# Causal attention and a gated unit on one core: a table of engine orders and choices replaced, 22 masks on GpSimd become 5

## The chip, the core and the metric

The kernel runs on one core of a Trainium2 chip. A core has five engines that run side by side, each through its own list of instructions in a fixed order: PE (TensorE, matrix products; its weight loads are a row of their own, PEld), DVE (VectorE), ACT (ScalarE), POOL (GpSimd) and SP (SyncE, which here issues the DMA transfers). An instruction waits until the instructions on other engines that it depends on have finished, and everything behind it on its engine waits with it. Products land in PSUM, eight banks of 512 fp32 per partition; PE writes them, ACT and DVE read them. In this kernel POOL works on SBUF alone.

The metric is device time in microseconds. Profile times are counted from the start of the profiled span.

## The reference

What is computed, with the setup and the types left out:

```python
def _attn_ref(q, k, v, s):                       # q, k, v: 8 x 8 x 576 x 64, s: 8 x 8 x 576
    scores = scale * np.matmul(q, k.transpose(0, 1, 3, 2))
    causal = np.triu(np.ones((S, S), dtype=bool), k=1)
    cum = np.cumsum(np.maximum(s, 0.0), axis=-1)
    bias = -(cum[:, :, :, None] - cum[:, :, None, :])
    scores = np.where(causal, -1000000000.0, scores + np.minimum(bias, 0.0))
    attn = np.exp(scores - np.max(scores, axis=-1, keepdims=True))
    attn = attn / (np.sum(attn, axis=-1, keepdims=True) + 1e-09)
    return np.matmul(attn, v)

def _moe_ref(x, w_val, conv_w, w_out):           # x: 8 x 576 x 512, the heads side by side
    xp = np.concatenate([np.zeros((B, K - 1, D)), x], axis=1)
    gate_pre = np.zeros((B, S, D))
    for k in range(K):                           # K = 5 taps
        gate_pre += conv_w[k][None, None, :] * xp[:, k:k + S, :]
    gate = 1.0 / (1.0 + np.exp(-gate_pre))
    return (gate * (x @ w_val)) @ w_out
```

## The kernel before

**Tiling.** The eight batches of eight heads are 32 units n = 4 b + p, each a batch b and a pair of heads p. The 576 positions fall in five key blocks of 128, 128, 128, 128 and 64. Because the bias is a difference of two cumulated sums, its row part falls away in the normalisation and its column part is a factor on v: `w` = exp(cum), and `vprime` writes Vp = v * w with a last column for the sum of each row.

**The steps of a unit.** q and k are loaded (`ld_q`, `ld_k`, the last 64 positions by `ld_t`), cast to bf16 (`c_q`, `c_k`), turned on PE (`qt`, `qq`, `tt`) and copied out of PSUM to the tiles QKT (`qe`, `te`). The scores come in three steps of 1024 columns for the two heads (`s0`, `s1`, `s2`, and `s4` for the last key block), each followed by one exp on ACT (`e0`, `e1`, `e2`, `e4`) into one of three buffers P. Step 0 holds the diagonal blocks. `av0` and `av` multiply P with Vp, 30 products of 65 columns; `rec` and `nm` normalise; `xt` turns the result and `xe` copies it out of PSUM to xT. The convolution is one start and three sums on a tile gp (`t1` to `t4`): on DVE a sum is one instruction, on POOL it needs a product first (`p2` to `p4`, into one of two buffers pr; such a product is sometimes made by ACT) and then an addition. `th` is the tanh of the gate, `val` the product with w_val, `glu` joins the two. `out` (128 rows each) is the product with w_out, `oe` copies it out of PSUM and `st` stores it. The last four units are split into a first part of 384 positions and a second of 192, with steps `u0` to `u3` and exps `f0` to `f3`, so that their products, sums and tanhs are of 384 and 192 columns.

**Two ways to mask.** The future positions of a diagonal block have to become zero. Either POOL writes zeros into P after the exp (`mk`, for the split units also `ml` for the second part: one affine select), or PE adds a large negative number to the scores ahead of the exp (`future`: two products with the tiles `fut`, one for each half of the rows, into the banks of step 0). Which one a unit gets follows from the table: where it names `mk.n`, unit n is masked on POOL, and else on PE.

**What sets the order.** One long table, `ORDER`, lists every step once, as name, engine and slots: `e` in `c_k.2:A:2` is A for ACT, V for DVE, G for POOL, T for PE, S for SP, and the rest names a PSUM bank, two banks, or a buffer. A loop at the end of `main_path` walks through it and emits each step; nothing reorders afterwards. So the table says for each engine in which order its work stands, which engine does a step that several can do, and in which bank or buffer. `wu` are products of the identity whose result nobody reads; they fill PE. All loads but the first two of k, and all stores, are issued by SP in the order of the table. The tiles `vst` of v are two, one for even and one for odd batches, so a load of v for batch b waits for the four `vp` of batch b - 2.

At the end `chk0` and `chk` reduce the reciprocals to a few flags on DVE, `cnt` counts them on PE, and every engine reads the count to decide whether `general_path`, a slower form that these inputs never need, has to run.

Of the kernel before, what the change touches and what calls it, by code (L numbers as in the profile page):

```python
# [16 lines left out]
B, H, S, D = 8, 8, 576, 64  # L17
# [175 lines left out]
ld_k.0.0:A ld_q.0.0:S ld_k.0.1:A wu.0:T:0 ld_t.0:S wu.1:T:7 wu.2:T:0 wu.3:T:7 ld_s:S wu.4:T:0 ld_q.0.1:S wu.5:T:7  # L193
wu.6:T:0 ld_q.0.2:S wu.7:T:7 c_k.0.0:V ld_k.0.2:S qt.0.0.k:T:0 wu.8:T:2 c_q.0.0:V ld_v.0.1:S qe.0.0.k:A qt.0.0.q:T:1
wu.9:T:7 c_k.0.1:G qe.0.0.q:A wu.10:T:2 wu.11:T:7 s0.0:T:0+1:0 e0.0:A tt.0:T:2 ld_q.0.3:S relu:V qt.0.1.k:T:3
wu.12:T:4 ld_k.0.3:S te.0:A wu.13:T:7 scan:V mk.0:G wu.14:T:0 ld_v.0.0:S qe.0.1.k:A s1.0:T:1+2 s4.0.0:T:4+5 c_q.0.1:A
s2.0:T:6+7 wu.15:T:0 c_q.0.2:G e1.0:A qt.0.1.q:T:3 wu.16:T:0 qe.0.1.q:V wu.17:T:0 wu.18:T:0 e4.0.0:A wu.19:T:0
centre:V s0.1:T:4+5:1 ld_k.1.0:S:2 s2.1:T:2+3 e0.1:A qt.0.2.q:T:1 c_k.0.2:V decT:T:0 ld_cw:S e2.0:A qt.0.2.k:T:4
mk.1:G wu.20:T:5 ld_k.1.1:S qe.0.2.k:V wu.21:T:5 wu.22:T:5 qe.0.2.q:A s1.1:T:6+7 c_k.0.3:V e2.1:A s0.2:T:4+5:2
c_q.0.3:G ld_v.0.2:S expw:A qt.0.3.q:T:1 e1.1:A s4.0.1:T:2+3 qe.0.3.q:V vp.0.0:G qt.0.3.k:T:0 qe.0.3.k:V e4.0.1:A  # L200
ld_q.1.0:S:3 e0.2:A s2.2:T:6+7 s1.2:T:2+3 vp.0.1:G av0.0:T:0+1 e2.2:A av.0:T ld_v.0.3:S mk.2:G rec.0:V av0.1:T:4+5
e1.2:A nm.0:V av.1:T c_k.1.0:G:2 s0.3:T:6+7:0 rec.1:V s2.3:T:2+3 e0.3:A nm.1:V ld_t.1:S cwT:T:0 xt.0:T:1 c_k.1.1:G
cwc:V xt.1:T:4 e2.3:A wu.23:T:6 xe.0:V ld_q.1.1:S vp.0.2:G qq.1.1:T:0:7 t1.0:V:0 s4.0.2:T:2+3 s1.3:T:5+6 e4.0.2:A
xe.1:V c_q.1.0:A:0 s4.0.3:T:2+3 mk.3:G t3.0:V ld_v.1.2:S e4.0.3:A t1.1:V:1 e1.3:A ld_v.1.1:S av0.2:T:2+3 vp.0.3:G
av.2:T t2.0:V ld_v.1.0:S qe.1.3:A tt.1:T:5 ld_v.1.3:S qe.1.2:V p4.1:G:0 p4.0:A:1 ld_v.1.4:S ld_wv:S:4 av0.3:T:6+7
av.3:T te.1:A rec.2:V ld_t.2:S t4.1:G c_q.1.1:G nm.2:V s0.6:T:0+1:1 rec.3:V xt.2:T:5 nm.3:V e0.6:A t4.0:G s0.7:T:2+3:2
xe.2:V s2.6:T:6+7 e0.7:A qq.1.0:T:0:1 t1.2:V:2 mk.6:G p2.1:A:0 s1.6:T:2+3 t3.2:V qe.1.0:A ld_q.2:S:0 mk.7:G qe.1.1:V
e2.6:A t3.1:V s1.4:T:0+1 e1.6:A s0.4:T:6+7:0 t2.2:V ld_k.2:S:1 xt.3:T:4 e0.4:A s0.5:T:2+3:0 t2.1:G t4.2:V s2.4:T:6+7
xe.3:V wu.24:T:5 e2.4:A vp.1.0:G mk.4:G wu.25:T:5 t1.3:V:3 wu.26:T:5 wu.27:T:5 ld_wo:S:2 wu.28:T:5 e1.4:A s4.1.3:T:6+7
ld_t.3:S t3.3:V wu.29:T:5 wu.30:T:5 e4.1.3:A s1.5:T:0+1 t4.3:V wu.31:T:5 th.2:A:0 ld_q.3:S:3 vp.1.2:G av0.4:T:6+7  # L210
th.1:A:1 av.4:T t2.3:V e0.5:A vp.1.1:G cast_wv:G rec.4:V av0.6:T:4+5 nm.4:V av.6:T e1.5:A s2.5:T:2+3 rec.6:V
s1.7:T:6+7 nm.6:V e2.5:A xt.4:T:0 ld_v.2.2:S c_q.2:G:1 tt.2:T:1 xe.4:V th.0:A:2 av0.5:T:2+3 t1.4:V:2 av.5:T te.2:A
ld_v.2.4:S val.3.0:T:4 th.3:A:3 p4.4:G:1 rec.5:V val.3.1:T:1 nm.5:V e1.7:A val.1.0:T:5 glu.3.0:V t4.4:G xt.5:T:2
c_k.2:A:2 glu.3.1:V ld_v.2.1:S val.1.1:T:3 glu.1.0:V s2.7:T:6+7 glu.1.1:V qq.2.0:T:1:5 vp.1.3:G xe.5:V val.0.0:T:3
# [82 lines left out]
def main_path(ctx, tc, q, k, v, s, moe_w_val, moe_conv_w, moe_w_out, out, okcnt):  # L297
# [44 lines left out]
    Ps = kind("P", [128, 2, 1536], BF16)  # L342
# [25 lines left out]
    at = {}  # L368
# [289 lines left out]
    def tap(m):  # L658
# [15 lines left out]
        return f  # L674

    split = lambda n: ("u0", n) in at

    def thof(n):
        return ths[at["th" if ("th", n) in at else "th0", n][0]].rearrange("p (h s) -> p h s", h=2)

# [159 lines left out]
```

## Time and profile before

| what | value |
|---|---|
| device time, three runs | 187.39, 188.7, 189.65 us; median 188.7 |
| span of the profiled execution | 187.6 us, 6637 instructions; the median of the runs is 1.1 above it |
| granted TensorE clock, mean | 0.999 |
| DMA | 40.46 MB, mean 216 GB/s |
| instructions of POOL that mask | 22 (18 of 1024 elements, 4 of 256) |

The device time of the profiled execution itself is not listed apart from the three runs. Its span, first to last instruction, is the time that the profile's rows divide up, and the sum below is made on it.

In the profile a row of the groups names the line, the engine, the operation, output and inputs, the shapes and the count; then the busy time, the mean length of one, and the engine's idle time just before these instructions with what ended it. Instructions of one engine overlap a little: a row of three exps lasts less than three times the length of one. L373 is the line of a helper that makes every copy and cast, so its groups are told apart by their tiles.

### The profile page before, as it was taken

The page shows a single profiled execution, that of the slowest core. Times are in us where ns is not written, and L with a number is a line of the kernel's source. Part 1 is how long each engine was busy: PE and PEld are TensorE (multiplying, and loading weights), DVE is VectorE, ACT ScalarE, POOL GpSimd, SP SyncE. Part 2 cuts the span into 40 slices and gives each one's busy share as a digit, 9 for nine tenths or more (in the row PEclk, how much of TensorE's full clock was granted, in tenths as well). Part 3 has the DMA queues.
Part 4 walks back from the last instruction along what each step waited for, and adds up shares of the span by engine and source line. Part 5 has one row for each costly group of instructions (what it writes and reads, how often), then busy time and mean ns, then how long its engine had stood idle before and what let it go on. Part 6 is the DMA issues. An engine that isn't in the chain of part 4 may idle for free.

```text
span 187.6 us, 6637 instructions
## 1 busy us (share of the span) xinstructions
PE 170.1 (91%) x2704; PEld 113.5 (60%) x2720; DVE 163.3 (87%) x321; ACT 170.6 (91%) x230; POOL 164.5 (88%) x149
## 2 busy tenths in 40 slices
PE   6898885888899998998978999999999999999991
PEld 2556573476757765576745667586566865776560
DVE  4355999878997899999999899998989899999980
ACT  2589899899999999999999999999999999999772
POOL 5267999899999999999978999999999989899610
PEclk9999999999999999999999999999999999999999
DMA  5998999999999999999298999899541003401164
GB/s 164 274 277 246 231 225 243 343 388 341 193 232 304 277 303 258 389 270 283 71 248 184 274 333 325 193 314 247 164 162 66 3 0 115 171 3 56 61 224 175
DMA packets 62283, 40.46 MB, mean 216 GB/s; under 512 B 47333, under 2 KB 49381, under 8 KB 62250
## 3 DMA queue, kind: packets, MB, share of 16 engines
q1 hardware_dynamic: 61706, 39.49, 77.1%
q8 instruction: 22, 0.36, 0.8%
q10 hardware_dynamic: 544, 0.52, 0.8%
q14 instruction: 11, 0.09, 0.2%
HBM read 30.57 MB, written 9.44 MB: 213 GB/s over the span
## 4 chain that ended last, share of the span: by engine, by line
PE 50%; ACT 15%; SPq 9%; DMA 8%; issue 6%; POOL 5%; DVE 4%; ACTq 0%; POOLq 0%; DVEq 0%
PE bank L723 14%; PE bank L703 11%; PE bank L594 10%; ACT P L556 9%; PE bank L505 7%; DMA vst<-in_v_dram 6%; SPq L435 3%; PE bank L629 3%; PE bank L626 3%; POOL gp L673 2%; DMA first<-in_k_dram 2%; ACT th L690 2%; SPq L471 2%; ACT QKT L373 2%; SPq L467 2%
## 5 line engine op out<-in xcount | busy, mean ns | idle before, releaser
L556 ACT ACTIVATE P<-bank 128x1024 bf16<-128x1024 f32 x84 | 82.9, 1042 | 4.1 <-PE bank L505 3.0
L670 DVE SCALAR_TENSOR_TENSOR gp<-bank,cwr,gp 128x574 f32<-128x574 bf16 (+6 forms) x72 | 52.3, 740 | 0.9 <-POOL gp L673 0.5
L673 POOL TENSOR_TENSOR gp<-gp,pr 128x572 f32<-128x572 f32 (+6 forms) x36 | 45.1, 1259 | 4.4 <-DVE gp L670 1.7
L474 POOL TENSOR_TENSOR Vp<-vst,w 128x650 bf16<-128x650 f32 x32 | 40.7, 1288 | 2.8 <-DMA vst<-in_v_dram 1.8
L505 PE MATMUL bank<-QKT 64*128 64x128 bf16 (+4 forms) x592 | 37.2, 237 | 4.8 <-ACT P L556 1.8
L703 PE MATMUL bank<-xT,wv 128*128 128x288 bf16 (+2 forms) x256 | 38.5, 287 | 1.1 <-ACT P L556 0.5
L594 PE MATMUL bank<-Vp,P 128*128 128x65 bf16 x960 | 36.0, 194 | 2.4 <-POOL Vp L474 1.1
L594 PEld LDWEIGHTS <-P 128*128 128x128 bf16 x960 | 33.2, 97 | 6.8 <-issue 1.5
L723 PE MATMUL bank<-wo,glu 128*128 128x512 bf16 x128 | 34.1, 380 | 1.5 <-issue 0.5
L505 PEld LDWEIGHTS <-QKT 64*128 64x128 bf16 x592 | 19.4, 94 | 22.3 <-issue 14.6
L712 DVE SCALAR_TENSOR_TENSOR glu<-th,bank 128x288 bf16<-128x288 f32 (+2 forms) x64 | 27.5, 445 | 2.0 <-ACT th L690 0.9
L703 PEld LDWEIGHTS <-wv 128*128 128x128 bf16 x256 | 22.4, 97 | 11.0 <-issue 4.8
L654 POOL TENSOR_TENSOR pr<-xT,cwr 128x572 f32<-128x572 bf16 (+6 forms) x28 | 28.3, 1020 | 0.6 <-ACT xT L373 0.6
L373 ACT COPY QKT<-bank 128x1024 bf16<-128x1024 bf16 (+1 forms) x26 | 24.2, 966 | 3.8 <-PE bank L489 2.9
L613 DVE TENSOR_TENSOR xn<-bank,recs 128x640 bf16<-128x640 f32 (+2 forms) x36 | 26.8, 745 | 0.6
L665 DVE SCALAR_TENSOR_TENSOR gp<-xT,cwr,bank 128x576 f32<-128x576 bf16 (+2 forms) x36 | 26.4, 741 | 0.7
L579 POOL TENSOR_SCALAR_AFFINE_SELECT P<-P 128x1024 bf16<-128x1024 bf16 (+1 forms) x22 | 22.3, 1021 | 4.2 <-ACT P L556 4.2
L690 ACT ACTIVATE th<-gp,cwr 128x576 f32<-128x576 f32 x28 | 22.0, 794 | 0.1
L723 PEld LDWEIGHTS <-glu 128*128 128x128 bf16 x144 | 12.4, 98 | 13.2 <-issue 1.6
L373 ACT COPY ot<-bank 128x512 f32<-128x512 f32 x26 | 15.2, 610 | 1.5 <-PE bank L723 1.0
L626 PE MATMUL bank<-ident,xn 128*128 128x128 bf16 x164 | 14.9, 219 | 0.7 <-ACT P L556 0.3
L373 POOL CAST qkb<-qkf 128x2048 bf16<-128x2048 f32 (+1 forms) x9 | 14.4, 1619 | 0.0
(66 smaller groups left out, 174.8 us busy)
## 6 DMA issues: line engine op xcount, KB each, us to landing
out_dram<-ot SPq DMA_DIRECT2D x36, 256.0 KB, 4.3
vst<-in_v_dram SPq DMA_DIRECT2D x28, 256.0 KB, 5.9
first<-in_q_dram SPq DMA_DIRECT2D x6, 512.0 KB, 6.0
first<-in_k_dram SPq DMA_DIRECT2D x6, 512.0 KB, 6.2
qkf<-in_q_dram SPq DMA_DIRECT2D x6, 512.0 KB, 6.7
qkf<-in_k_dram SPq DMA_DIRECT2D x6, 512.0 KB, 7.3
vst<-in_v_dram SPq DMA_DIRECT2D x15, 128.0 KB, 5.4
first<-in_q_dram SPq DMA_DIRECT2D x4, 256.0 KB, 5.3
```

The lines of the kernel that those rows point to most:

```text
L373: (act.copy if e is act else e.tensor_copy)(dst, src)
L474: e.tensor_tensor(Vps[b % 2][:, :, HP[p]], vslot(b)[:, :, HP[p]], w[:, :, b * 8 + 2 * p:b * 8 + 2 * p + 2].unsqueeze(3).to_broadcast([128, ...
L505: pe.matmul(ps[:, hh, c0:c0 + nq], QKTs[b % 2][r, 1, p, k0:k0 + 128], QKTs[b % 2][r, 0, p, q0:q0 + nq], **kw)
L556: act.activation(out=Pt(n)[:, :, step * 512:(step + 1) * 512], in_=pair((f"s{step}", n)), func=AF.Exp, scale=0.125)
L594: pe.matmul(ps[:, o:o + 65], lhsT, Vps[b % 2][:, kb, 2 * p + w, :], start=(kb == 0), stop=(kb == qb))
L613: vec.tensor_tensor(xns[b % 2][:, g, p * 128:(p + 1) * 128].rearrange("t g (w d) -> t w g d", w=2), ps[:, :, :, 0:64], recs[:, n, :, g].un ...
L654: pool.tensor_tensor(pr, xTs[b % 2][:, c, 4 + lo - m:4 + hi - m], r.to_broadcast([128, hi - lo]), ALU.mult)
L670: vec.scalar_tensor_tensor(gp[:, lo:hi], xps(n, *h)[:, lo - m:hi - m], r, gp[:, lo:hi], ALU.mult, ALU.add)
L673: pool.tensor_tensor(gp[:, lo:hi], gp[:, lo:hi], prs[at[f"p{m}", n, *h][0]][:, lo:hi], ALU.add)
L703: pe.matmul(ps, wv[:, dc, c * 128:(c + 1) * 128], xTs[b % 2][:, dc, 4 + lo:4 + hi], start=(dc == 0), stop=(dc == 3))
L712: vec.scalar_tensor_tensor(glu2[:, c, o + lo:o + hi], th[:, lo:hi], 1.0, ps, ALU.add, ALU.mult)
L723: pe.matmul(bank_of(u, i), glu2[:, c, i * 128:i * 128 + 128], wo[:, c, :], start=(c == 0), stop=(c == 3))
```

## The change

The table `ORDER` is replaced. Loads and stores are issued by SP in the same sequence as before. By engine, the steps that another engine does now, or that are there in another number:

| step | before | after |
|---|---|---|
| masks on POOL, `mk` / `ml` | 18 / 4 | 5 (units 11, 17, 22, 25 and the split unit 29) / 0 |
| units whose step 0 is masked on PE, of the 28 whole ones | 10 | 24 |
| fillers `wu` on PE | 32 | 50 |
| casts `c_k.2`, `c_k.0.2`, `c_k.1.0`, `c_q.0.1` | ACT, DVE, POOL, ACT | POOL, ACT, ACT, POOL |
| tap products on POOL, whole / half | 20 / 8 | 21 / 10 |
| tap products on ACT, whole / half | 7 / 1 | 5 / 2 |
| tap sums on POOL, whole / half | 27 / 9 | 26 / 12 |
| tap sums on DVE, whole / half | 57 / 15 | 58 / 12 |
| `qe` on ACT, DVE | 26, 10 | 28, 8 |
| `oe` on ACT, DVE | 26, 10 | 28, 8 |
| `te` on ACT, DVE | 6, 2 | 4, 4 |
| `xe` on ACT, DVE | 12, 24 | 10, 26 |
| `chk0` on DVE | behind `nm.27`, among the tap sums of unit 24 | behind the last `glu` |

The first rows of the table in the diff, and what else it changes (a buffer P is now named where the first exp of a unit writes it, since its three steps no longer come in one order):

```diff
 ORDER = """
-ld_k.0.0:A ld_q.0.0:S ld_k.0.1:A wu.0:T:0 ld_t.0:S wu.1:T:7 wu.2:T:0 wu.3:T:7 ld_s:S wu.4:T:0 ld_q.0.1:S wu.5:T:7
+ld_q.0.0:S ld_k.0.0:A ld_k.0.1:A ld_t.0:S ld_s:S ld_q.0.1:S ld_q.0.2:S ld_k.0.2:S c_q.0.0:V ld_v.0.1:S c_k.0.0:V
...
-    Pt = lambda n, h=None: Ps[at["s0" if h is None else f"u{2 * h}", n][1]]
+    split = lambda n: n in splits
+
+    def Pt(n, h=None):
+        steps = ("e0", "e1", "e2") if h is None else (f"f{2 * h}", f"f{2 * h + 1}")
+        return Ps[next(at[f, n] for f in steps if (f, n) in at)[0]]
...
-            split = ("u0", n) in at
-            g = ((3, 1)[h] if split else 4)
+            g = ((3, 1)[h] if split(n) else 4)
...
+    splits = {int(name.split(".")[1]) for name, *_ in steps if name.startswith("u0.")}
```

Three places of the new order. First POOL, from its first cast of the inputs to the v of batch 0 (Vp0, from the buffer vst0). L579 is the mask; it stands in the new file on L586, L373 on L377, L474 on L478. Before:

```order
L373 CAST qkb1_103<-first_91 128x2x4x64
L579 AFFINE_SELECT P0_116<-P0_116 128x2x512
L373 CAST qkb0_102<-first_91 128x2x4x64
L579 AFFINE_SELECT P1_117<-P1_117 128x2x512
L373 CAST qkb0_102<-first_91 128x2x4x64
L474 TENSOR_TENSOR Vp0_109<-vst0_92,w_140 128x5x130 x2
L579 AFFINE_SELECT P2_118<-P2_118 128x2x512
L373 CAST qkb2_104<-qkf0_136 128x2x8x64 x2
```

and after:

```order
L377 CAST qkb1_103<-first_91 128x2x4x64
L377 CAST qkb0_102<-first_91 128x2x4x64 x2
L478 TENSOR_TENSOR Vp0_109<-vst0_92,w_140 128x5x130
L377 CAST qkb0_102<-first_91 128x2x4x64
L478 TENSOR_TENSOR Vp0_109<-vst0_92,w_140 128x5x130
L377 CAST qkb2_104<-qkf0_136 128x2x8x64
L478 TENSOR_TENSOR Vp0_109<-vst0_92,w_140 128x5x130 x2
L377 CAST qkb1_103<-qkf1_137 128x2x8x64
```

The three masks between are gone from POOL, and so the casts of q and k and the Vp of batch 0 follow one another.

The second place is POOL from the v of batch 3 (Vp1, from the buffer vst1) to the k of batch 6. `gp` is a tap sum, `pr` a tap product, the casts to qkb take q and k of later batches. Before:

```order
L474 TENSOR_TENSOR Vp1_110<-vst1_93,w_140 128x5x130 x2
L579 AFFINE_SELECT P0_116<-P0_116 128x2x512
L579 AFFINE_SELECT P2_118<-P2_118 128x2x512
L373 CAST qkb0_102<-qkf2_138 128x4x8x64
L474 TENSOR_TENSOR Vp1_110<-vst1_93,w_140 128x5x130
L579 AFFINE_SELECT P1_117<-P1_117 128x2x512
L373 CAST qkb1_103<-qkf0_136 128x4x8x64
L373 CAST qkb2_104<-qkf1_137 128x4x8x64
L673 TENSOR_TENSOR gp2_121<-gp2_121,pr0_134 128x572
L474 TENSOR_TENSOR Vp1_110<-vst1_93,w_140 128x5x130
```

and after:

```order
L377 CAST qkb2_104<-first_91 128x4x8x64
L478 TENSOR_TENSOR Vp1_110<-vst1_93,w_140 128x5x130 x4
L377 CAST qkb1_103<-qkf0_136 128x4x8x64
L377 CAST qkb0_102<-qkf1_137 128x4x8x64
L377 CAST qkb2_104<-qkf2_138 128x4x8x64
L377 CAST qkb1_103<-first_91 128x4x8x64
L680 TENSOR_TENSOR gp3_122<-gp3_122,pr1_135 128x572
L661 TENSOR_TENSOR pr0_134<-xT1_114,cwr_144 128x572
```

The four Vp of batch 3, which stood apart with three masks, three casts and a tap sum between them, are one row, and the cast of k of batch 6 (qkb1 from the tile first) has come ahead of the tap sum of unit 13 (in the new table `t4.13`, the row of gp3).

The third place is the end of DVE, from the last `glu`. `okt`, `stat` and `ok` are the flags, `okcnt` their count. Before:

```order
L712 SCALAR_TENSOR_TENSOR glu2_115<-th3_126,bank_153 128x192
L712 SCALAR_TENSOR_TENSOR glu2_115<-th1_124,bank_153 128x192
L734 TENSOR_REDUCE stat_149<-recs_141 128x1
L735 TENSOR_REDUCE stat_149<-recs_141 128x1
L745 TENSOR_SCALAR ok_148<-stat_149 128x2
L746 TENSOR_SCALAR ok_148<-stat_149 128x2
L758 TENSOR_REDUCE okcnt_58<-bank_153 1x1
```

and after:

```order
L716 SCALAR_TENSOR_TENSOR glu2_115<-th2_125,bank_153 128x192
L716 SCALAR_TENSOR_TENSOR glu2_115<-th0_123,bank_153 128x192
L716 SCALAR_TENSOR_TENSOR glu2_115<-th3_126,bank_153 128x192
L743 TENSOR_TENSOR okt_150<-cwr_144 128x20
L744 TENSOR_SCALAR ok_148<-okt_150 128x20
L738 TENSOR_REDUCE stat_149<-recs_141 128x1
L739 TENSOR_REDUCE stat_149<-recs_141 128x1
```

The last four of these rows are `chk0`; it now stands between the last `glu` and `chk`, whose five rows follow as before.

## The prediction on record

> **What bounds the kernel now.** I read the page's busy times first, then six stretches, then the waits and the chain, and last single instructions. The busy times:
>
> ```profile
> PE 170.1 (91%) x2704; PEld 113.5 (60%) x2720; DVE 163.3 (87%) x321; ACT 170.6 (91%) x230; POOL 164.5 (88%) x149
> ```
>
> Four engines are at 87 to 91%, so an average tells nothing about which one holds the end. The stretches (width, then busy time of PE, PEld, DVE, ACT, POOL with instruction counts, granted clock, DMA share, GB/s) do:
>
> ```profile
> 0.00:10.00 10.00, 8.03 (x51) 3.73 (x51) 4.61 (x15) 4.61 (x7) 4.32 (x14) 1.00 0.88 221
> 10.00:40.00 30.00, 24.56 (x453) 16.63 (x452) 24.71 (x43) 27.43 (x37) 26.36 (x24) 1.00 1.02 272
> 40.00:90.00 50.00, 47.22 (x811) 32.34 (x815) 45.73 (x84) 48.95 (x60) 49.77 (x38) 1.00 1.10 289
> 90.00:160.00 70.00, 67.00 (x1126) 45.57 (x1127) 66.41 (x120) 68.44 (x91) 67.11 (x53) 1.00 0.64 178
> 160.00:173.00 13.00, 12.95 (x198) 9.26 (x198) 12.73 (x34) 12.53 (x21) 12.35 (x16) 1.00 0.22 79
> 173.00:188.00 15.00, 10.33 (x92) 5.95 (x90) 9.10 (x30) 8.68 (x19) 4.58 (x9) 0.98 0.40 144
> ```
>
> From 40 to 90 us POOL is the fullest: it idles 50.00 - 49.77 = 0.23 us, ACT 1.05. From 90 to 160 ACT is the fullest (idle 1.56; POOL 2.89). Between 10 and 173 us ACT idles 2.57 + 1.05 + 1.56 + 0.47 = 5.65 us in all. So two engines bound the middle, POOL first and ACT about 1 us behind it. PE is the fullest only from 160 on. The loads bound the first 34 us, and the chain shows it:
>
> ```profile
> 28.08 5.99 DMA vst<-in_v_dram
> ...
> 34.23 1.28 POOL Vp L474
> 35.51 1.06 POOL P L579
> 36.61 1.11 PE bank L594 x30
> ```
>
> The v of batch 1 is issued at 28.08, lands at 34, is scaled by POOL, and then a POOL mask (L579, 1.06 us) stands between it and the PE products that need both.
>
> **The change, part by part.** The prices of the moved work are these groups (busy us, mean ns of one):
>
> ```profile
> L579 POOL TENSOR_SCALAR_AFFINE_SELECT P<-P 128x1024 bf16<-128x1024 bf16 x18 | 20.6, 1153 | 4.2 <-ACT P L556 4.2
> ...
> L579 POOL TENSOR_SCALAR_AFFINE_SELECT P<-P 128x256 bf16<-128x256 bf16 x4 | 1.7, 426 | 0.0
> ...
> L373 POOL CAST qkb<-first 128x2048 bf16<-128x2048 f32 x5 | 9.5, 1896 | 0.0
> ...
> L654 POOL TENSOR_TENSOR pr<-xT,cwr 128x572 f32<-128x572 bf16 x9 | 10.3, 1147 | 0.2 <-ACT xT L373 0.2
> ...
> L673 POOL TENSOR_TENSOR gp<-gp,pr 128x572 f32<-128x572 f32 x13 | 18.3, 1406 | 1.7 <-DVE gp L670 1.3
> ...
> L620 PE MATMUL bank<-ident 128*128 128x512 bf16 x32 | 10.7, 451 | 1.4 <-POOL ident masks.py:199 1.4
> ...
> L518 PE MATMUL bank<-fut,fut 64*128 64x512 bf16 x20 | 3.8, 376 | 0.0
> ```
>
> *Masks off POOL.* Eighteen full masks cost 20.6 us, 1.14 each; four small ones 1.7. Four full ones stay and one of 768 elements is new, which I put between 0.43 and 1.14 in proportion to its elements, at 0.9. That is 4 x 1.14 + 0.9 = 5.5 in place of 22.3, so -16.8 us. POOL takes in return one whole cast of k (1.9) and loses a half one while gaining a small one (together +1.5), and, by the table of counts, one full tap product more and one full tap sum fewer (1.15 - 1.41 = -0.3), two half products and three half sums more (about 0.64 each, between half and two thirds of the rows L654 and L673: +3.2). That is +2.9. Sum: -12.4 us, POOL from 164.5 to about 152.
>
> *Masks onto PE.* Fourteen more score groups get the pair of `fut` products. Ten pairs take 3.8 us now, 0.38 a pair with their drain. A product of 512 columns in a run takes 0.22:
>
> ```profile
> 54.27 1.73 PE bank L723 x8
> ```
>
> (1.73 / 8). The two of a pair lie on the two halves of the rows, so a pair costs 0.22 to 0.38, and the fourteen 3.1 to 5.3 us of PE. Four masks of the split steps move as well, each a pair of 128 columns, under 0.1 us. Eighteen more filler products (L620, 10.7 / 32 = 0.33 each) add 6.0 us of busy PE, and in the order all but two stand ahead of the first output products, where PE has idle time (24.56 of 30.00 busy between 10 and 40 us). I cost them at nothing; their cover is that idle time, and if it is gone they cost up to 6. PE's cover for the masks is that its groups run with drain between them; the waits say how often ACT really stands for its scores:
>
> ```profile
> ACT P L556 <- PE bank L505: 3.0, 7, 0.7
> ...
> POOL P L579 <- ACT P L556: 4.2, 2, 2.6
> ...
> DVE recs L607 <- PE bank L594: 5.0, 9, 1.4
> ```
>
> Three us in 84 exps: PE is mostly ahead of ACT. I take 0 for the masks on the path and keep +5.3 as the upper end; below nothing there is a gain, since the mask's 1.1 us leaves the path from exp to the value products (the 1.06 at 35.51 above).
>
> *ACT.* The exps and tanhs do not change in number. What moves on or off:
>
> ```profile
> L373 ACT COPY QKT<-bank 128x1024 bf16<-128x1024 bf16 x22 | 21.8, 1034 | 0.7 <-PE bank L629 0.6
> ...
> L373 ACT COPY ot<-bank 128x512 f32<-128x512 f32 x26 | 15.2, 610 | 1.5 <-PE bank L723 1.0 <-ACT ot L373 0.6
> ...
> L373 ACT CAST QKT<-bank 128x512 bf16<-128x512 f32 x6 | 3.6, 606 | 0.4 <-PE bank L480 0.4
> ...
> L373 ACT CAST qkb<-first 128x2048 bf16<-128x2048 f32 x1 | 1.9, 1898 | 0.0
> ...
> L373 ACT CAST qkb<-qkf 128x1024 bf16<-128x1024 f32 x1 | 1.0, 1037 | 0.0
> ...
> L373 ACT COPY QKT<-bank 128x512 bf16<-128x512 bf16 x4 | 2.4, 592 | 3.0 <-PE bank L489 2.9
> ...
> L652 ACT ACTIVATE pr<-bank,cwr 128x572 f32<-128x572 bf16 x4 | 3.2, 789 | 0.0
> ...
> L373 ACT COPY xT<-bank 128x576 bf16<-128x576 bf16 x7 | 4.6, 656 | 0.0
> ```
>
> One big cast leaves, one half comes: -1.90 + 1.04. Two evacuations of QKT come, one whole, one small: +1.03 + 0.59. Two of the outputs come, +1.22; two tails leave, -1.21. One copy of xT leaves, -0.66. Two whole tap products leave and a half one comes, about -0.9. Sum -0.8 us. DVE loses two output copies, two QKT copies and half a cast, gains two tails and a copy of xT: about -2.5 us, on an engine that idles 3.6 us between 90 and 160; I take nothing for it.
>
> *v of batch 3 and the SP queue.* SP issues in order. Its own timeline and POOL's:
>
> ```profile
> 85.32 0.63 SPq L731 DMA_DIRECT2D out_dram<-ot  x1
> ...
> 92.41 0.99 SPq L471 DMA_DIRECT2D vst<-in_v_dram  x2
> ...
> 91.06 1.32 POOL L474 TENSOR_TENSOR Vp<-vst,w 128x650 bf16<-128x650 f32 x1
> ...
> 98.97 1.28 POOL L474 TENSOR_TENSOR Vp<-vst,w 128x650 bf16<-128x650 f32 x1 [0.88 <-DMA vst<-in_v_dram]
> ```
>
> From 85.95 to 92.41 SP stands before the first v of batch 5, since that buffer is free only when POOL has made the last Vp of batch 3, at 91.06. Behind it in the queue is the last v of batch 4, so POOL waits for that until 98.97. The change makes all four Vp of batch 3 in one piece ahead of the casts, so the 6.5 us of SP go. What is late next is one row further in POOL's new order: the cast of k of batch 6, now ahead of the tap sum that was at 89.71. The second half of its load is issued only at 82.67 here, and such loads take 7.3 us to landing (the last number of the second row):
>
> ```profile
> 82.67 0.63 SPq L435 DMA_DIRECT2D first<-in_k_dram  x1
> ...
> qkf<-in_k_dram SPq DMA_DIRECT2D x6, 512.0 KB, 7.3
> ```
>
> So that cast starts no earlier than 82.67 + 7.3 = 90, and everything behind it on POOL waits: what POOL saves before 90 us can't be carried past that row whole. So I take the gain from ACT's idle time and none from POOL's 12.4 us as such.
>
> *The check of the sums* moves to the end of DVE's order. It costs four short instructions, the longest of them
>
> ```profile
> L734 DVE TENSOR_REDUCE stat<-recs 128x1 f32<-128x280 f32 x1 | 0.4, 437 | 0.0
> ...
> 182.37 0.17 DVE L746 TENSOR_SCALAR ok<-stat 128x2 bf16<-128x2 f32 x1
> ...
> 183.37 0.17 PE L749 MATMUL bank<-ok,onec 128*1 128x24 bf16 x1
> ```
>
> With two such reductions and two smaller ones some 1.2 us. The count that follows was ready at 182.54 and ran at 183.37 behind the last output products, so 0.8 is covered. I take 0 and keep +0.4.
>
> *The sum.* On the profiled span of 187.6: -0.8 (ACT's own work) and -1.7, which is 30% of ACT's idle 5.65 us. I choose 30% because POOL, whose fullness feeds part of those waits, is relieved before 90 us alone by the full amount, and the loads hold one place of it. That gives 185.1. The median of the three runs is 1.1 above the span, so 186.2. The ends: all of the 5.65 gone, 187.6 - 0.8 - 5.65 = 181.2, with the 1.1 182.3; and all fourteen pairs on the path at 0.38, 188.7 - 0.8 + 5.3 = 193.2.
>
> [...]
>
> **The rivals.**
>
> 1. *ACT and the loads hold it.* POOL's idle time grows and nothing else moves: 188.7 - 0.8 = 187.9. For it: ACT idles just 1.05 and 1.56 us in the two long stretches, and SP's row at 82.67. Against it: POOL idles 0.23 between 40 and 90, less than ACT.
> 2. *Slower: masks on PE ahead of the exps.* PE works in order, and the pair now sits between the scores and ACT's exp of the diagonal step. It decides from the point where PE comes to that group no earlier than ACT does; then each pair is ACT's wait. Fourteen at 0.22 to 0.38, less 0.8: 191.0 to 193.2. For it: PE has half of the chain below, and 12.95 of 13.00 us from 160 on. Against it: the 3.0 us that ACT waited in all.
>
> ```profile
> PE 50%; ACT 15%; SPq 9%; DMA 8%; issue 6%; POOL 5%; DVE 4%; ACTq 0%; POOLq 0%; DVEq 0%
> ```
>
> 3. *Much faster.* POOL was the bound through the first half and its waits end everywhere: all of ACT's idle time goes, 182.3 to 184.
>
> **How the numbers follow.** About 1% is what a measurement of this kernel can tell from no change: the three runs lie between 187.39 and 189.65. The forecast has 0.45, around 186.2 (185.0 to 187.3), four fifths of it below 186.8; rival 1 has 0.22 at 187.9, rival 2 0.20 from 190 on, rival 3 0.13. Faster by over 1%: 0.36 + 0.13 = 0.49. Within 1%: 0.09 + 0.22 + 0.04 = 0.35. Slower by over 1%: 0.16. The range from 183.0 to 190.9 leaves out half of rival 3 and a good half of rival 2, some 0.18.
>
> **What would show it.** Right: POOL's busy time near 152; L579 at five instructions; no SP wait of 6 us for Vp; ACT's idle time between 10 and 173 us about 4; ACT's waits for L505 still near 3 us. Rival 1: ACT's idle time as now, and POOL's waits on the k loads in its place. Rival 2: ACT's waits for PE by L505 or L518 over 6 us. Wrong altogether: new waits of ACT for DVE or POOL where the new order sets a step just behind its source, which no row here can show.

## The result and the profile after

The changed kernel takes 194.5 us (median of four runs, 194.04 to 195.03) against 188.62 for the kernel before on the same chip: a ratio of 1.030, interval 1.025 to 1.035. It is 5.9 us slower; the forecast was 186.2, and its range ended at 190.9. The profiled execution has a span of 193.15 us, 5.6 more than the 187.57 of before. Medians, ratios and intervals in this document are over fast runs; a run more than 1.5% above the fastest of its kernel counts as slow and is left out.

The changed kernel's page, busy time by engine:

```profile
PE 176.0 (91%) x2754; PEld 115.4 (60%) x2772; DVE 165.3 (86%) x318; ACT 170.0 (88%) x229; POOL 153.3 (79%) x138
```

POOL lost 11.2 us of work and ACT 0.6, and yet the span grew: the relief did not reach the end. The six stretches of the changed kernel (width, then busy time of PE, PEld, DVE, ACT, POOL with counts, granted clock, DMA share, GB/s):

```profile
0.00:10.00 10.00, 8.48 (x56) 4.12 (x56) 4.03 (x15) 3.86 (x5) 4.07 (x15) 1.00 0.88 223
10.00:40.00 30.00, 26.88 (x469) 17.13 (x462) 24.25 (x42) 28.51 (x38) 17.70 (x16) 1.00 1.00 275
40.00:90.00 50.00, 47.96 (x823) 32.72 (x828) 45.88 (x80) 47.84 (x62) 44.35 (x32) 1.00 1.02 281
90.00:160.00 70.00, 66.21 (x1114) 44.38 (x1116) 65.62 (x115) 66.10 (x86) 65.31 (x52) 1.00 0.65 174
160.00:173.00 13.00, 12.84 (x181) 8.77 (x180) 12.75 (x30) 12.71 (x21) 11.34 (x11) 1.00 0.28 102
173.00:188.00 15.00, 13.65 (x146) 8.24 (x147) 12.75 (x41) 10.96 (x22) 10.58 (x17) 1.00 0.38 141
```

The reader should follow ACT, the fourth of the busy times. Its idle time is 1.49 us from 10 to 40 (2.57 before), then 2.16 (1.05), 3.90 (1.56) and 0.29 (0.47): 7.84 us in place of 5.65. It gains 1.1 us early and loses 3.5 between 40 and 160. What it waits for is in the list of waits (engine, line and what ended the wait: us in all, times, longest):

```profile
ACT P L564 <- PE bank L509: 3.2, 5, 1.2
...
ACT P L564 <- PE bank L522: 1.9, 3, 0.8
...
ACT P L536 <- PE bank L522: 1.0, 3, 0.5
```

L564 and L536 are exps, L509 the scores and L522 the mask products. The exps wait 6.1 us for PE in 11 waits, 3.2 us of it for scores and 2.9 for mask products; before, they waited 3.0 for the scores, L505. The chain has moved to PE and DVE and no longer runs over SP and DMA:

```profile
PE 54%; DVE 19%; ACT 9%; issue 8%; POOL 7%; POOLq 0%; DVEq 0%; ACTq 0%
```

The rest of the loss lies behind the last work. Before, PE's branch past `general_path` (L807) began at 184.65 and the span ended 2.92 us later. In the changed kernel (L812) it began at 188.21, and the end came 4.94 us later. The branch of each engine in the changed kernel; the three numbers in ns are the shortest, the median and the longest:

```profile
L812 ACTq COMPARE_BRANCH  x1: 45/45/45, 188.1 to 188.1; - x1
L812 POOLq COMPARE_BRANCH  x1: 45/45/45, 188.2 to 188.2; - x1
L812 DVEq COMPARE_BRANCH  x1: 72/72/72, 188.2 to 188.2; - x1
L812 PEldq COMPARE_BRANCH  x1: 3898/3898/3898, 188.2 to 188.2; - x1
```

and PE's in the kernel before:

```profile
L807 PEldq COMPARE_BRANCH  x1: 358/358/358, 184.7 to 184.7; - x1
```

So the 5.6 us of span are 3.6 by which PE reaches its branch later, and 2.0 behind that.

### The profile page after: what moved, and what is told of

Same layout as the page of the kernel before. It is cut to its first block, busy times and chain, and to the rows that moved or that the text cites. A ratio compares the mean times of both kernels' runs of the same rounds, so it can differ in the third digit from the quotient of the medians.

```text
span 193.1 us, 6754 instructions
## 1 busy us (share of the span) xinstructions
PE 176.0 (91%) x2754; PEld 115.4 (60%) x2772; DVE 165.3 (86%) x318; ACT 170.0 (88%) x229; POOL 153.3 (79%) x138
## 4 chain that ended last, share of the span: by engine, by line
PE 54%; DVE 19%; ACT 9%; issue 8%; POOL 7%; POOLq 0%; DVEq 0%; ACTq 0%
PE bank L601 11%; PE bank L727 10%; PE bank L707 10%; PE bank L509 9%; DVE gp L677 6%; ACT P L564 5%; DVE gp L672 4%; POOL gp L680 3%; PE bank L633 3%; PE bank L636 3%; PE bank L627 3%; DVE glu L716 3%; DVE xn L620 2%; POOL pr L661 2%; PE bank L522 2%
## 5 line engine op out<-in xcount | busy, mean ns | idle before, releaser
L564 ACT ACTIVATE P<-bank 128x1024 bf16<-128x1024 f32 x84 | 81.7, 1043 | 5.6 <-PE bank L509 3.2
L677 DVE SCALAR_TENSOR_TENSOR gp<-bank,cwr,gp 128x574 f32<-128x574 bf16 (+5 forms) x70 | 53.2, 761 | 1.8
L478 POOL TENSOR_TENSOR Vp<-vst,w 128x650 bf16<-128x650 f32 x32 | 40.5, 1284 | 5.4 <-DVE QKT L377 3.9
L509 PE MATMUL bank<-QKT 64*128 64x128 bf16 (+5 forms) x592 | 37.8, 237 | 3.3 <-ACT P L564 2.5
L707 PE MATMUL bank<-xT,wv 128*128 128x288 bf16 (+2 forms) x256 | 37.0, 286 | 0.8 <-ACT P L564 0.6
L661 POOL TENSOR_TENSOR pr<-xT,cwr 128x572 f32<-128x572 bf16 (+6 forms) x31 | 30.4, 985 | 6.8 <-DVE xT L377 4.9
L601 PE MATMUL bank<-Vp,P 128*128 128x65 bf16 x960 | 34.2, 194 | 0.2 <-POOL Vp L478 0.2
L601 PEld LDWEIGHTS <-P 128*128 128x128 bf16 x960 | 31.9, 98 | 4.2 <-issue 1.4
L509 PEld LDWEIGHTS <-QKT 64*128 64x128 bf16 x592 | 20.1, 94 | 22.1 <-issue 15.4
L377 ACT COPY QKT<-bank 128x1024 bf16<-128x1024 bf16 (+1 forms) x28 | 25.9, 974 | 3.5 <-PE bank L493 3.3
L716 DVE SCALAR_TENSOR_TENSOR glu<-th,bank 128x288 bf16<-128x288 f32 (+2 forms) x64 | 26.1, 448 | 2.7 <-PE bank L707 1.6
L377 POOL CAST qkb<-first 128x2048 bf16<-128x2048 f32 (+1 forms) x10 | 14.0, 1402 | 8.0 <-DMA first<-in_q_dram 3.0
L377 POOL CAST qkb<-qkf 128x2048 bf16<-128x2048 f32 (+1 forms) x8 | 13.4, 1677 | 5.0 <-PE bank L484 2.9
L627 PE MATMUL bank<-ident 128*128 128x512 bf16 x50 | 15.8, 432 | 1.4 <-POOL ident masks.py:199 1.4
L377 ACT COPY ot<-bank 128x512 f32<-128x512 f32 x28 | 16.2, 606 | 0.9 <-PE bank L727 0.7
```

The lines of the kernel that those rows point to most:

```text
L377: (act.copy if e is act else e.tensor_copy)(dst, src)
L478: e.tensor_tensor(Vps[b % 2][:, :, HP[p]], vslot(b)[:, :, HP[p]], w[:, :, b * 8 + 2 * p:b * 8 + 2 * p + 2].unsqueeze(3).to_broadcast([128, ...
L509: pe.matmul(ps[:, hh, c0:c0 + nq], QKTs[b % 2][r, 1, p, k0:k0 + 128], QKTs[b % 2][r, 0, p, q0:q0 + nq], **kw)
L564: act.activation(out=Pt(n)[:, :, step * 512:(step + 1) * 512], in_=pair((f"s{step}", n)), func=AF.Exp, scale=0.125)
L601: pe.matmul(ps[:, o:o + 65], lhsT, Vps[b % 2][:, kb, 2 * p + w, :], start=(kb == 0), stop=(kb == qb))
L661: pool.tensor_tensor(pr, xTs[b % 2][:, c, 4 + lo - m:4 + hi - m], r.to_broadcast([128, hi - lo]), ALU.mult)
```

## The experiments

All times are medians beside the kernel before on the same chip; ratios are to that kernel, with a 95% interval. "Delay" below is the start of a batch's exps (those of the last key block apart) in a profiled execution less that of the same exps in the kernel before, as a mean. It compares one execution with one, and is good to about 1 us: two traces of the changed order, with the dear and the cheap branch of the next section, have delays of 3.32 and 2.25 us at the last `glu`, ahead of that branch. The trace of before is also of a long execution. In all runs whose span is on record the device time is 1.66 to 2.23 us above the span, so the span of 187.57 belongs to the longest run of before, 189.65, and against its median the delays would be some 1 us larger.

### The branch at the end

The edit is the same in both kernels: a filler becomes four products of 128 columns, the same 512 columns for PE in more instructions; in the kernel before PE comes to its branch at 184.5 us with them and at 184.65 without.

```diff
+SPLIT = (0, 1, 2, 3, 4, 5, 6, 7)
...
     def unread(e, i):
+        if i in SPLIT:
+            for j in range(4):
+                pe.matmul(bank[:, at["wu", i][0], 128 * j:128 * j + 128], ident, ident, start=True, stop=True)
+            return
```

In the kernel before (fillers 0 to 16):

> The kernel before, with its first 17 fillers each issued as four products of 128 columns and no longer as one of 512: the same PE work and order, 102 more PE instructions, so that the last branch of PE stands 5515 instructions into its program, 5413 in before and 5518 in the changed kernel. Theory 'place of the branch': the 3.9 us that PE's compare-and-branch takes at the end of the changed kernel (0.36 us in before) hangs on how many PE instructions stand ahead of it. Then this kernel's branch takes 3 to 4 us too and the time is 190.7 us, 2.1 over before (189.8 to 191.2). Rival 'the check at the end': the branch is slow because the changed kernel has its first checks (chk0) at the end, or for its data; then the branch takes 0.4 us here and the time is 188.6 (188.0 to 189.2).

In the changed kernel (fillers 0 to 7, as in the diff):

> The changed kernel with its first 8 fillers split in the same way: 48 more PE instructions, the branch at 5566. In the trace of the changed kernel a 16 KB fetch of PE instructions came about every 256 of them, the last ones after some 5288 and 5540. Theory 'place of the branch': with the branch past 5540 the next block has been fetched ahead of it, so that the branch takes 0.4 us again: 192.4 us, 2.1 under the changed kernel (191.9 to 192.9). Theory that only the count matters, the more the slower: no gain, 194.5. Rival 'the check at the end': 194.5 (194.0 to 195.0).

Measured: 190.68 us, 1.0108 (1.0057 to 1.0158), and 191.92 us, 1.0205 (1.0151 to 1.0259). Each came out where the first theory had it. PE's branch in the kernel before with 102 more instructions:

```profile
L812 PEldq COMPARE_BRANCH  x1: 4158/4158/4158, 184.5 to 184.5; - x1
```

and in the changed kernel with 48 more:

```profile
L817 PEldq COMPARE_BRANCH  x1: 445/445/445, 187.2 to 187.2; - x1
```

The same code, at the same time in the program and with the same data, takes over ten times as long with the branch behind 5515 instructions as behind 5413, and is cheap again behind 5566. That is a loss of 2.0 us by the spans, and a third of the whole. `chk0` has no part in it, as it stands early in the first of the two and late in the second. All kernels below have their branch at a place known to be cheap (behind 5566 to 5571) or dear (5515 to 5518), nearly all by split fillers. Those in the changed order are read against 1.0205 or 1.0301 accordingly, those in before's order against 1 or 1.0108.

### Masks: from GpSimd to PE, and back

First before's table with its masks as in the changed kernel.

```diff
-mk.0:G ... mk.27:G ml.28:G ml.29:G ml.30:G ml.31:G
+mk.11:G mk.17:G mk.22:G mk.25:G mk.29:G
```

> The kernel before with its masks where the changed kernel has them (units 17, 25 and the first half of 29 to GpSimd; 0 to 4, 6, 7, 9, 12 to 14, 18 to 20, 24, 27 and the second halves of 28 to 31 to PE), all else in before's order; 6 fillers split, so that the branch stands at 5517 as in the kernel with 17 split, against which it is read. Theory 'masks': the mask products on PE make the exponentials late by most of the 3.4 us that the changed kernel loses ahead of its end: +2 to +4 us over the kernel with 17 fillers split, 192.7 to 194.7 if the branch costs 2.1 us. Rival 'order': the loss comes from the new order of the engines, and the masks alone move the time by no more than 0.7 us either way, or make it shorter since GpSimd has 15 us less to do: 189.5 to 191.4 with the dear branch.

Measured: 192.98 us, 1.0249 (1.0185 to 1.0314), 2.3 us over its partner with the dear branch. The sum falls on the side of the masks, but the trace shows no delay of the exps of batches 1 to 6 (between -0.9 and +0.1 us against its partner), and then one wait: ACT stands 1.25 us ahead of the first exp of unit 31, which starts at 164.46, 1.6 later than in the partner. PE had stood still there, for a mask that this kernel adds on GpSimd:

```profile
L594 PE MATMUL bank<-Vp,P 128*128 128x65 bf16 x960 | 35.7, 194 | 2.3 <-POOL P L579 1.1
```

So the run put a price on two things at once. The next leaves the three added masks on PE:

```diff
-mk.17:G mk.25:G mk.29:G
```

> The kernel before with 20 masks taken from GpSimd to PE (units 0 to 4, 6, 7, 9, 12 to 14, 18 to 20, 24, 27 and the second halves of 28 to 31), as in the changed kernel, and none put on GpSimd in their place: in the run that had three more there, the only late wait against its partner was 1.36 us ahead of the first exponential of unit 31's first half. 13 fillers are split, so that the branch stands at 5571, where it was cheap. Theory 'order': PE's mask products are covered in before's order, and GpSimd's 20 masks less shorten nothing: 188.6 (188.0 to 189.2). Rival 'masks': the products cost time wherever they stand, 190.4 to 191.5.

Measured over 12 runs: 190.24 us, 1.0059 (1.0029 to 1.0089), 1.1 us, between the two theories. Its stretches from 40 to 173 us:

```profile
40.00:90.00 50.00, 48.45 (x816) 32.57 (x817) 45.74 (x83) 48.90 (x60) 44.26 (x33) 1.00 1.02 275
90.00:160.00 70.00, 68.08 (x1149) 45.79 (x1143) 66.09 (x120) 68.38 (x91) 61.60 (x48) 1.00 0.65 182
160.00:173.00 13.00, 13.00 (x202) 9.03 (x196) 12.56 (x33) 12.47 (x20) 12.02 (x13) 1.00 0.24 84
```

POOL has 5.5 us less in the first of them and as much less in the second, and ACT does no more than before: 48.90 against 48.95, 68.38 against 68.44. This is the balance of both, of POOL's relief and PE's added work. That POOL at 50 of 50 us was full and held hardly anybody up stands in before's own list of waits between 40 and 90 us, where these are all that POOL ended; ACT waited for it nowhere:

```profile
PE bank L594 <- POOL Vp L474: 0.7, 1, 0.7
...
DVE gp L670 <- POOL gp L673: 0.5, 1, 0.5
...
PE bank L723 <- POOL wo L373: 0.3, 1, 0.3
```

The other way round, the changed kernel with before's masks on GpSimd (the mask of unit 3 comes behind that unit's first value product here, so part of its future positions are left in):

```diff
-mk.17:G mk.25:G mk.29:G
+mk.0:G ... mk.27:G ml.28:G ml.29:G ml.30:G ml.31:G
```

> The changed kernel with the masks where before has them (22 on GpSimd), all else in its own order; 11 fillers split, so that the branch stands at 5517 (5518 in the changed kernel, which it is read against). Theory 'masks': 3.4 us less 0.7 at most is won back, 191 to 192.3. Rival 'order': the time stays at 194.5 (193.8 to 195.2), or is longer, since this order was made for a GpSimd with 15 us less to do: up to 198.

Measured: 205.72 us, 1.0908 (1.0855 to 1.0961), beyond both theories. The value products wait for the masks:

```profile
L603 PE MATMUL bank<-Vp,P 128*128 128x65 bf16 x960 | 35.7, 195 | 10.5 <-POOL P L588 10.2 <-POOL Vp L480 0.2
```

The new order puts a unit's value products close behind its exps, with no room for a mask between. The run tells nothing of what the mask products cost. So the next leaves the work out altogether:

```diff
-            score_products(..., step == 0 and ("mk", n) not in on_pool)
+            score_products(..., step == 0 and ("mk", n) not in on_pool and n not in NO_MASK)
...
-                           j == 0 and (("mk", "ml")[h], n) not in on_pool)
+                           j == 0 and h == 0 and ("mk", n) not in on_pool)
```

> The changed kernel without the mask products of the 20 units and halves that the change moved to PE: their future scores are left in, so that the output isn't the reference's; no engine does the work. 13 fillers split, the branch at 5516, dear as in the changed kernel. Theory 'order': the waits of ACT for PE lie where scores stand behind other work, and only the two or three of them that have a mask product just ahead get shorter: 193.4 to 194.5. Rival 'masks': 191 to 192, all but 0.7 of the 3.4 us won back.

Measured: 193.73 us, 1.0225 (1.0163 to 1.0287), 0.76% under the changed kernel, though the two intervals overlap. By the profile the span is 1.3 us shorter. ACT's waits are still there:

```profile
ACT P L566 <- PE bank L511: 4.1, 8, 0.9
...
ACT P L538 <- PE bank L524: 1.0, 3, 0.5
```

5.1 us, after 6.1 with the products: most of ACT's waiting for PE stays without them. Its delays, in the table below, are those of the changed kernel with the cheap branch to within 0.25 us in every batch and at the last `glu`. So the price of the masks, 1.1 us in before's order, lies in the changed order between next to nothing (by the trace) and 1.4 us (by the medians), and what the changed kernel loses up to batch 3 is not theirs.

### Fillers

The changed kernel without its fillers from number 22 on:

```diff
-wu.22:T:3 ... wu.49:T:7
```

> The changed kernel without its fillers from number 22 on (28 of the 50; before has 32, 9 of them in that stretch), 9 of the first split, the branch at 5516. Theory 'order': they stand where PE waits anyhow, 194.5 (193.9 to 195.1). Rival 'fillers': 18 more at 0.22 us are 4 us of PE work, and taking away 28 wins back 2 to 3.4 us: 191 to 192.5. Second rival: the granted clock falls in the stretch without them, and the time is 195 to 198.

Measured: 195.91 and 197.86 us, a median of 196.9, 4.1% over before's 189.12, as the second rival had it; two runs allow no interval. The granted clock (behind the five busy times) falls between 10 and 40 us:

```profile
10.00:40.00 30.00, 22.80 (x419) 16.17 (x417) 22.83 (x39) 28.03 (x38) 19.25 (x17) 0.87 0.94 257
```

In this order the fillers can't be spared, and the run can't tell what they cost. The converse puts the changed kernel's fillers into before's table, each ahead of the same PE step:

```diff
-wu.23:T:6 ... wu.31:T:5
+wu.23:T:2 ... wu.50:T:3
```

> The kernel before with the changed kernel's fillers: its own 9 from the stretch after 20 us out, 28 put in, each ahead of the same PE step as in the changed kernel and into a bank that is free there: 51 fillers, 19 more than before, some 4 us of PE work at 0.22 us each. Masks and order as before; 20 fillers split, the branch at 5571, where it was cheap. Theory 'fillers': PE has no 4 us to spare, 1.008 to 1.015 over before. Theory 'order': they fill PE's waits of the first 40 us, 0.997 to 1.004.

And with the 20 masks on PE as well:

> The kernel before with both kinds of work that the change gives PE: the 51 fillers of the other kernel of this pair, and 20 masks on PE (1.0059 by themselves); order, banks and engines of all else as before, the branch at 5567. The changed kernel with a cheap branch stands at 1.0205. If PE's added work is the loss: 1.016 to 1.022. If it is the order with its waits: 1.004 to 1.010, and 1.0 to 1.6% are left to the order.

Measured: 193.8 us, 1.026 (1.0215 to 1.0305), and 196.48 us, 1.0417 (1.0356 to 1.0479). Both lie beyond what either theory gave. Fillers are not free in before's order: they cost 4.9 us, more than their own 4. But the banks that were free for them there make them wait for ACT to read those, for longer than the whole loss:

```profile
L631 PE MATMUL bank<-ident 128*128 128x512 bf16 x31 | 9.0, 380 | 5.3 <-ACT P L564 4.0 <-ACT QKT L377 1.1 <-ACT P L536 0.2
```

In the changed kernel only the first of its fillers waits (1.4 us, for the identity), so 4.9 is not what they cost there. But the pair tells two things. The masks cost 1.1 us alone, and on top of the fillers some 3.0 by the ratios (1.57%) and 2.2 by the delay at the last `glu`. The intervals are wide for such a difference, but it fits a slack of PE that can be spent once. And the delays show that most of what is lost stays lost:

| delay, us, in batch | 0 | 1 | 2 | 3 | 4 | 5 | 6 | 7 | last `glu` |
|---|---|---|---|---|---|---|---|---|---|
| 51 fillers | -0.35 | 1.45 | 4.30 | 4.46 | 4.23 | 4.25 | 4.24 | 4.24 | 4.25 |
| 20 masks on PE | 0.36 | 0.46 | -0.43 | 0.02 | -0.25 | -0.07 | 0.15 | 0.41 | 0.55 |
| masks and fillers | -0.13 | 1.89 | 4.83 | 5.48 | 5.45 | 5.80 | 6.02 | 6.28 | 6.42 |
| changed kernel | 0.53 | 0.58 | 0.81 | 2.16 | 2.82 | 3.06 | 2.48 | 1.28 | 3.32 |
| changed kernel, cheap branch | 0.37 | 0.42 | 0.65 | 2.00 | 1.74 | 1.98 | 1.41 | 0.21 | 2.25 |
| changed, no mask products | 0.37 | 0.41 | 0.63 | 1.96 | 1.82 | 1.80 | 1.20 | -0.01 | 2.02 |

In the first row before's order wins back 0.2 of 4.46 us behind batch 3, and from batch 4 on the delay is constant to 0.02 us. In the last three rows a batch's exps stand in another order than in before, so that small steps from batch to batch say little.

### Two scores earlier

```diff
-av.5:T:6+7 ... av0.5:T:6+7 ... s2.7:T:4+5
+s2.7:T:4+5 av.5:T:6+7 ... av0.5:T:6+7
...
-av0.12:T:6+7 ... av.12:T:6+7 th.13:A:1 s0.17:T:0+1
+s0.17:T:0+1 av0.12:T:6+7 ... av.12:T:6+7 th.13:A:1
```

> The changed kernel with two score steps of PE put earlier in the same order: those of unit 7's third column (s2.7) ahead of the value products of unit 5's other head, and those of unit 17's first column (s0.17) ahead of the value products of unit 12; nothing else, the branch at 5518. In the changed kernel ACT waits 1.06 us for the one and 1.31 for the other while PE does value products. Theory 'order': the waits shrink by 0.35 (the bank is free only when DVE has read it) and by 1.0, and the time by most of it: 193.3 (192.9 to 193.8). Rival 'too much work on PE': PE has no time to spare, what is put behind is late next, and the time stays at 194.5 (194.1 to 194.9).

Measured: 195.3 us, 1.0327 (1.0266 to 1.0388): no gain, the rival's outcome. ACT around the second of the two exps, that of s0.17, in the changed kernel; L377 copies output, L564 is the exp:

```profile
95.32 0.59 ACT L377 COPY ot<-bank 128x512 f32<-128x512 f32 x1
97.12 1.02 ACT L564 ACTIVATE P<-bank 128x1024 bf16<-128x1024 f32 x1 [1.21 <-PE bank L509]
98.08 0.58 ACT L377 COPY ot<-bank 128x512 f32<-128x512 f32 x1
98.74 1.02 ACT L564 ACTIVATE P<-bank 128x1024 bf16<-128x1024 f32 x1
```

and with the scores moved:

```profile
96.14 1.02 ACT L563 ACTIVATE P<-bank 128x1024 bf16<-128x1024 f32 x1 [0.29 <-PE bank L508]
98.03 0.59 ACT L376 COPY ot<-bank 128x512 f32<-128x512 f32 x1 [0.86 <-DMA vst<-in_v_dram]
98.69 1.02 ACT L563 ACTIVATE P<-bank 128x1024 bf16<-128x1024 f32 x1
```

The exp starts 0.98 us earlier and the next exp 0.05. The wait has gone over to the copy between, whose product PE ends at 97.99; in the changed kernel it ends at 98.05. (The row names a load.) PE itself has no gap there, in the changed kernel:

```profile
93.89 1.03 PE L727 MATMUL bank<-wo,glu 128*128 128x512 bf16 x4
94.75 2.00 PE L601 MATMUL bank<-Vp,P 128*128 128x65 bf16 x60
96.68 0.40 PE L509 MATMUL bank<-QKT 64*128 64x128 bf16 x8
97.01 1.04 PE L727 MATMUL bank<-wo,glu 128*128 128x512 bf16 x3
```

### Seams between the two orders

To find the place of what is left, seven kernels take one table up to a point and the other for all steps left, with a cheap branch. The edit, for the seam at 89 us:

```diff
 ORDER = """
+ld_k.0.0:A ... t4.13:G qq.4.1:T:5:3
+qe.4.1:A ... st.3.7:S flag:S
```

The first line is before's table to `qq.4.1`, the second the changed table without the steps done.

> Before's order, engines, banks, masks and fillers for the steps that before issues in its first 37 us, and the changed kernel's for all steps left, in its order. 17 fillers split, so that PE's branch stands at 5569, where it was cheap; the changed kernel with a cheap branch was 2.05% over before. Three theories for these 3.9 us, for four such kernels with the seam at 37, 89, 133 and 161 us: 'fixed places' (each stretch of the new order has waits of its own for ACT; by ACT's busy time up to the seam in before, less that of the changed kernel with a cheap branch, the losses ahead of 37, 89, 133 and 161 us are none, 25%, 54% and 90%); 'debt' (the masks and fillers that PE got in the first 90 us make it late for the rest); 'tail' (the new order of the last batch costs 1 to 2 us by itself). Here: fixed places 2.0% over before (1.6 to 2.4); debt 1.0 to 2.0; tail 2.0.

> As the kernel with the seam at 37 us, with the seam at 89 us (the tile of three output rows is taken from another of the six buffers where both orders would use one at a time). 21 fillers split, the branch at 5567. Fixed places: 1.55% over before (1.1 to 2.0); debt: 0 to 0.5%, since PE's added work of the first 90 us is gone; tail: 1.5 to 2.0.

> As the kernel with the seam at 37 us, with the seam at 133 us. 23 fillers split, the branch at 5567. Fixed places: 0.95% over before (0.5 to 1.4); debt: 0 to 0.3%; tail: 1.0 to 1.5.

> As the kernel with the seam at 37 us, with the seam at 161 us: the changed kernel's order is left for the last batch's halves, the output products and the checks at the end. 23 fillers split, the branch at 5567. Fixed places: 0.2% over before (-0.3 to 0.6); debt: 0; tail: 0.6 to 1.2.

The other way round:

> The seam the other way round: the changed kernel's order, engines, banks, masks and fillers for the steps that it issues in its first 37 us, and before's for the rest; 18 fillers split, the branch at 5568, where it was cheap. By ACT's busy time up to there (29.53 us in the changed kernel with a cheap branch, 29.36 in before) the new start wins 0.2 us. Theory 'the tail is most of it' (the kernel with the seam at 161 us lost 1.39% of the changed kernel's 2.05 with a cheap branch): this one is as fast as before, ratio 0.997 to 1.003. Rival 'the masks and fillers of the start leave a debt': 1.008 to 1.015.

> As the kernel with the changed start, with the seam at 87 us: the new order of batches 1 to 3 is in, with 12 of the 20 masks on PE and 48 of its fillers. Branch at 5568. Theory 'the tail is most of it': ACT has done 0.6 to 0.8 us less work by then than in before, 1.003 to 1.006. Rival 'debt': 1.010 to 1.020.

> As the kernel with the changed start, with the seam at 172 us: all of the changed kernel but its last steps (two exponentials, the second halves of the last batch with their taps and gates, the last output products, the checks). Branch at 5568. If the last steps themselves (taps of the second halves on GpSimd, 6 of 12 in before's engines) are the tail's loss: 1.004 to 1.010. If the tail loses between 161 and 172 us, by what stands ahead of the last exponentials on ACT and PE: 1.015 to 1.022, as the changed kernel with a cheap branch (1.0205).

And the seam at 161 us with four masks back on GpSimd:

> The kernel with the seam at 161 us (1.0139) with the masks of the second halves of units 28 to 31 on GpSimd as before, all else of the changed tail. Branch at 5569. Theory 'mask products in the tail': ACT's wait of 0.57 us for the last exponential and PE's 0.9 us of products go, 1.008 to 1.011. Rival 'order and engines of the tail': 1.012 to 1.020, since GpSimd, which ends 4.4 us later there than in before, gets 1.7 us more to do.

| kernel | median, us | ratio, interval | delay in batch 2 | 3 | 5 | 7 | last `glu` |
|---|---|---|---|---|---|---|---|
| before to 37 | 193.12 | 1.0247 (1.0185-1.0308) | 2.75 | 4.11 | 3.33 | 1.56 | 3.59 |
| before to 89 | 192.05 | 1.0190 (1.0107-1.0272) | -0.45 | -0.20 | 2.21 | 0.42 | 2.47 |
| before to 133 | 191.64 | 1.0174 (1.0102-1.0247) | -0.16 | 0.36 | -0.27 | 0.18 | 2.22 |
| before to 161 | 191.59 | 1.0139 (1.0092-1.0186) | 0.85 | 0.95 | 0.44 | 1.74 | 2.72 |
| changed to 37 | 192.08 | 1.0188 (1.0150-1.0227) | 3.24 | 3.25 | 2.86 | 2.87 | 2.87 |
| changed to 87 | 192.24 | 1.0209 (1.0160-1.0258) | 0.69 | 2.10 | 2.32 | 2.33 | 2.33 |
| changed to 172 | 193.28 | 1.0250 (1.0202-1.0298) | 0.44 | 1.79 | 2.52 | 0.72 | 4.01 |
| 161, masks back | 192.41 | 1.0204 (1.0154-1.0254) | 0.13 | 0.13 | -0.43 | 0.91 | 2.73 |

Wherever the seam lies, and whichever order comes first, 1.4 to 2.5% are lost, and the delay appears just behind the seam, but for the kernel changed to 87 us. The kernel with 37 us of the new order should have been as fast as before by the theory of the tail and 0.8 to 1.5% slower by that of the debt; it lost 1.9%, and 3.2 us by batch 2. The parts don't add up, so a seam costs about as much as what it was to place, and these runs can't divide the rest of the loss between the stretches. Two things can be read from them. Up to batch 3 the kernel changed to 87 us runs as the changed kernel does (0.69 and 2.10 against 0.65 and 2.00), and before's order then carries the delay of 2.1 to 2.3 us to the end: a loss of this size is present in the first 87 us of the new order. And moving the masks of the second halves back to POOL wins nothing, as the last row is no faster than its partner; POOL gets their work there, so that the products themselves have no price from it.

## Why the prediction was wrong

*POOL.* 152 us were forecast and 153.3 measured; five masks are left and the wait of SP is gone (the v of batch 5 is issued at 88.62, not 92.41). ACT's own work fell by 0.6 for the forecast 0.8. The bookkeeping held. DVE's busy time rose by 2.0 us where 2.5 less was forecast, but busy time counts overlapping instructions once: the lengths of DVE's instructions add up to 181.2 us before and 179.6 after, 1.6 less. They overlap less in the new order.

*"I choose 30%": the gain of 1.7 us.* This is the first step that failed. It read POOL's 0.23 us of idle time between 40 and 90 as a bound. The kernel with 20 masks moved and nothing else has 5.5 us more idle time on POOL in that stretch and ACT is no faster by any of it, and in before's own trace PE waits 1.0 us for POOL there, DVE 0.5 and ACT none. Rival 1 was right in this: POOL was full and hardly in anyone's way. In place of the gain, ACT's idle time between 10 and 173 us rose from 5.65 to 7.84.

*"I take 0 for the masks on the path."* Twenty of them cost 0.59% in before's order, 1.1 us, and between nothing and 1.4 us in the new one: above zero in the first, and far under the 5.3 of the upper end in both. The reason given, that ACT waited just 3.0 us for scores, shows that PE was ahead, not that it had time to spare: 67.00 of 70.00 us were busy from 90 to 160 and 12.95 of 13.00 behind that. The row of the weight loads stood at 60%, and the twenty masks cost 0.59% all the same.

*"I cost the fillers at nothing; their cover is that idle time."* In before's order it isn't there: 19 more cost 4.9 us, with 5.3 us of waits for banks among their rows. What they cost in the changed kernel, which is built around them, no run could isolate.

*The end.* The working has a term of 0 to 0.4 us for the check of the sums and none for the branch. From the start of the last `glu` to PE's branch it is 2.88 us before and 3.12 after, so the check's term was right. The branch behind it cost 2.0 us more of the span, by its place in the program alone (it took 3.90 us, and 0.45 with 48 instructions more ahead of it). Nothing in the profile of before shows that place to be critical, but the count of PE's instructions was there to be compared.

*Rival 2* had a time of 191.0 to 193.2, and with a cheap branch the changed kernel takes 191.92; its mark, over 6 us of ACT waiting for scores and masks, is met with 6.1. Both are luck. It put 3.1 to 5.3 us on the mask products as ACT's waits, where the runs give 1.1 for 20 masks in before's order and 1.4 at most in the new one, and 5.1 of the 6.1 us of waits stay when the products are left out. What is right in it is the engine: ACT waits longer for PE, but mostly for scores (4.1 of those 5.1).

*The balance.* Of 3.0%, 1.0% is the branch, which is shown. The masks are 0.6% in before's order, which is shown too; in the new order their share lies between nothing and 0.8%. The other 1.3 to 2.0%, 2.4 to 3.9 us, is open between the 18 fillers more and the order with its choice of banks. In the trace 43 of the 50 fillers stand ahead of 37 us, and the exps of batch 2, which before starts from 51 to 70 us, are just 0.65 to 0.81 us late; the 2 us come with batch 3, when only three fillers are left, one at 67.9 us and two at 101.5. That speaks for the order, but no run tested it. ACT's idle time shows seven waits of 0.3 to 1.2 us between 40 and 160 us, six for PE and one for DVE; moving two of the scores behind them brought nothing, so the places are known and the cause isn't. No version tried was faster than the kernel before.

## What to carry to other kernels

An engine without a gap in a stretch is not thereby the bound (POOL, busy for 49.77 of 50.00 us, was relieved of 5.5 and ACT gained nothing): ask who waits for it, and take its work away in the old order before an order is built upon that. Slack seems to be spent once here, so several edits that each lie "in PE's idle time" have to be costed together, and where a delay of the first 60 us reaches the end nearly whole there was little. Where a program ends in a branch, compare its place in the instruction stream when instructions are added ahead of it: 102 more took the branch from 0.36 to 4.16 us here, and 48 more took it from 3.90 to 0.45.

## What was not expected of the hardware

DMA queue q8, which the page lists as "instruction", moves packets of 16,384 bytes, 22 in the kernel before and 23 in the changed one. In these two traces, up to the branch, one starts for every 254 PE instructions on the mean, with 134 to 381 between two. In the seven kernels whose branch stands behind 5515 to 5518 instructions it took 3.8 to 4.2 us. In each of them a packet started 0.9 to 1.5 us into the branch, the one before it having started 13 to 15 us ahead of the branch (0.94 and 13.5 us in the changed kernel). In the kernels with 5413, or with 5566 to 5571, it took 0.35 to 0.46 us, and a packet had started 4 to 11 us ahead of it (10.7 in the kernel before). The price is some 3.5 us of the branch (3.90 against 0.36) and 2.0 of the span. That a long branch waits for the packet that starts in it is the author's reading of these times; the runs show only how its length goes with its place.

The granted clock fell where PE had less to do: with 28 fillers fewer, PE was busy 22.80 of 30.00 us between 10 and 40 in place of 26.88, and the clock was 0.87 there, 0.60 between 30 and 40. Busy time alone doesn't fix it. In kernels with before's order in that stretch the traces show 1.00 with 24.56 us busy (before) and 0.94 with 25.17 (before to 133) and 24.29 (before, 17 fillers split).
